# Gate maxima through ScalarE's DMA queue, zero products between the first fold products, and a new instruction order

## The chip, the cores and the metric

The kernel runs on one core of a Trainium2 chip. TensorE (PE) multiplies matrices; VectorE (DVE), ScalarE (ACT) and GpSimd (POOL) do the elementwise work; SyncE (SP) issues nearly all DMA transfers. Each engine works through its own list of instructions in order, and waits where an operand is not ready. The metric is the device time of one execution in microseconds, as a median of several runs.

## The reference, cut to what matters

Three stages follow each other: a gated recurrence over 768 steps for 4 batches of 8 heads, a first feed-forward block, and a second one.

```python
for t in range(S):                       # S = 768, per batch and head, D = 40
    m_new = max(f[t] + m, i[t])          # the running gate maximum
    C = exp(f[t]+m-m_new) * C + exp(i[t]-m_new) * outer(v[t], k[t])
    n = exp(f[t]+m-m_new) * n + exp(i[t]-m_new) * k[t]
    m = m_new
    y[t] = sigmoid(o[t]) * (C @ q[t]) / max(abs(n @ q[t]), 1)
x = y.reshape(3072, 320)
h = ((x @ w1) * (x @ w2)) @ w3           # d_ff = 1024
x = h @ w_out
h = max(x @ v1, x @ v2, x @ v3)          # d_ff = 768
out = h @ v_out
```

The first block multiplies by w3 and then by w_out. Nothing stands between the two, so the kernel computes `w3 @ w_out` once, and uses the product.

## The kernel before, in words

**The recurrence** is cut into chunks of 87 steps, nine per batch (36 in all). A *visit* (`visit`, L817) computes on PE the scores of one chunk (s, L839) and, from the state, the output of the chunk before it (o, L848). VectorE multiplies the scores by a table of decays (`pk`, L873), and the next visit reads the result. The decays of the first nine chunks (`decay`, L744) are made on PE (L757, L758) from the tables `hl` and `one`, and ScalarE takes their exponential (`dd`, L761).

**The gates** come first (L533 to L652). The gate inputs `gi` are loaded, VectorE scans them (L574, L585), joins the chunks (L607, L612) and leaves the maxima in `gft`. These stand with the heads on the partitions, and `hl` wants the chunks there. So they are written to DRAM in three stores (L619) and read back in one load (L650). ScalarE rounds the loaded piece into `hl` (L651) and VectorE adds the remainder (L652). Both DMAs are on SP's queue.

**The fold** (`fold`, L1227) computes `w3 @ w_out` in eight parts of eight products of 320 columns (L1236). The weights arrive as 64-bit floats in *granules* (`granule`, L1154): a DMA, a scaling of the upper word on ScalarE (Prelu, L1172), a shift of the lower word on VectorE (L1181) or on ScalarE (L1178), and a merge on VectorE (L1189). `w_out` has five granules (`wof`, all parts need them), each part has two of w3, and the first of the first part comes in two halves. The landing buffers are four called `sx` and three called `stg`, and the merged halves of w3 go to five buffers `w_0` to `w_4`.

**The rest of PE's work** (L970 to L1102) is the two blocks, in seven blocks of tokens. It starts when the first five chunks are through.

**At the very start** PE multiplies zeros by zeros (`warm`, L508: sixteen, then six more before the first fold product), so that PE is busy while the weights travel.

**What sets the order:** the program is written as a list of operations with their dependencies. A planner (`Plan.run`, L254) plays it with a cost for each operation. Among the operations that are ready on an engine it takes the one with the lowest number in the table `PRIO`, and where an operation may run on either of two engines, the table `PICK` says on which. `WARM` is the time up to which the planner counts PE as slow. What comes out is a fixed list of instructions for each engine.

Of the kernel before, what the change touches and what calls it, by code (L numbers as in the profile page):

```python
# [65 lines left out]
    "11100111101000000100000110110011111101101111000111010011000110011110110011001110001111001011111110110000110010"  # L66
    "00001011101000111101100110011001101110001010010110011101001010110010111001101100101001110001001000001011111011"
    "10100110000001001110000011011110000100011011010111000100110110100000010000000000100100101000010100111101100110"
    "01000100010000101100001100010011010100110011110001011100000110011001110010111000000"
)  # L70
PRIO = (
# [95 lines left out]
)  # L167
WARM = 11500
USTEPS = (
    (0, 1, 3, 5, 8, 11, 14, 18, 22, 26), (0, 2, 4, 6, 8, 11, 14, 17, 20, 23, 26), (0, 2, 4, 6, 8, 9, 11, 12, 14, 15)  # L170
)
# [192 lines left out]
def mlstm_moe_kernel(  # L364
# [133 lines left out]
    def T(*key):  # L498
        v = made[key]
        return v() if callable(v) else v  # L500
# [966 lines left out]
```

## Time and profile before

| | |
|---|---|
| Time before, median of 3 runs | 662.33 us (662.04 to 665.41) |
| The profiled execution | 666.85 us, of which the span is 665.1 us |
| PE busy | 650.4 us, 98% of the span |
| DVE, ACT, POOL busy | 345.7, 296.4, 215.1 us |
| DMA, mean over the span | 114 GB/s |

The span runs from the first instruction to the last. A busy PE can still be slow: the profile also gives the clock that PE was granted. The time between the profiled execution and the median (4.5 us) is no part of any stage, so differences are worked out in the profile and carried over to the median.

### The profile page before, as it was taken

The page shows a single profiled execution, that of the slowest core. Times are in us where ns is not written, and L with a number is a line of the kernel's source. Part 1 is how long each engine was busy: PE and PEld are TensorE (multiplying, and loading weights), DVE is VectorE, ACT ScalarE, POOL GpSimd, SP SyncE. Part 2 cuts the span into 40 slices and gives each one's busy share as a digit, 9 for nine tenths or more (in the row PEclk, how much of TensorE's full clock was granted, in tenths as well). Part 3 has the DMA queues.
Part 4 walks back from the last instruction along what each step waited for, and adds up shares of the span by engine and source line. Part 5 has one row for each costly group of instructions (what it writes and reads, how often), then busy time and mean ns, then how long its engine had stood idle before and what let it go on. Part 6 is the DMA issues. An engine that isn't in the chain of part 4 may idle for free.

```text
span 665.1 us, 14153 instructions
## 1 busy us (share of the span) xinstructions
PE 650.4 (98%) x5903; PEld 575.0 (86%) x5903; DVE 345.7 (52%) x623; ACT 296.4 (45%) x578; POOL 215.1 (32%) x235
## 2 busy tenths in 40 slices
PE   7799999999999999999999999999999999999997
PEld 5477799999999999999999987788788888888896
DVE  5579899877853673554553354464632311332222
ACT  7756986686723353453432343553331122322031
POOL 4053454665512324343244433463300013010030
PEclk9999999999999999999999999999999999999999
DMA  8989964645411444433123244342000010000011
GB/s 277 341 307 369 332 209 150 214 136 186 141 59 62 135 152 147 116 96 90 50 72 104 91 152 127 108 149 65 1 1 1 0 40 1 0 1 0 1 40 39
DMA packets 25457, 75.92 MB, mean 114 GB/s; under 512 B 3145, under 2 KB 6217, under 8 KB 25394
## 3 DMA queue, kind: packets, MB, share of 16 engines
q1 hardware_dynamic: 25394, 75.02, 34.3%
q8 instruction: 46, 0.75, 0.5%
q14 instruction: 17, 0.14, 0.1%
HBM read 70.98 MB, written 4.03 MB: 113 GB/s over the span
## 4 chain that ended last, share of the span: by engine, by line
PE 83%; DVE 5%; DMA 5%; ACT 2%; issue 2%; POOL 1%; SPq 0%; POOLq 0%; ACTq 0%; DVEq 0%
PE wk L970 13%; PE wk L971 13%; PE wk L972 13%; PE wk L973 6%; PE acs L1102 6%; PE wk L975 5%; PE acs L1082 3%; PE acs L1084 3%; PE acs L1086 3%; PE wk L1236 3%; PE aq L848 3%; PE ac L1102 3%; PE aq L839 2%; DMA sx<-in_w3t 2%; PE wk L985 2%
## 5 line engine op out<-in xcount | busy, mean ns | idle before, releaser
L1049 DVE TENSOR_TENSOR misc<-misc,wk 128x384 f32<-128x384 f32 (+2 forms) x87 | 51.3, 594 | 130.5 <-PE wk L975 96.7
L997 ACT CAST hp<-misc 128x384 fp32r<-128x384 f32 (+2 forms) x101 | 55.0, 547 | 141.5 <-DVE misc L1049 53.1
L1001 POOL TENSOR_TENSOR hp<-misc,hp 128x384 fp32r<-128x384 f32 (+1 forms) x40 | 45.6, 1140 | 119.2 <-ACT hp L997 109.3
L970 PE MATMUL wk<-xx,wch 128*128 128x384 f32 (+1 forms) x216 | 77.3, 358 | 0.3 <-DVE misc L1049 0.3
L971 PE MATMUL wk<-xx,wcl 128*128 128x384 f32 (+1 forms) x216 | 76.6, 355 | 0.0
L972 PE MATMUL wk<-xx,wch 128*128 128x384 f32 (+1 forms) x216 | 76.5, 354 | 0.0
L1019 DVE TENSOR_TENSOR misc<-misc,wk 128x384 f32<-128x384 f32 (+1 forms) x56 | 33.8, 607 | 76.8 <-ACT misc L1017 52.2
L970 PE MATMUL wk<-xx,wah 128*128 128x384 f32 (+1 forms) x192 | 69.8, 364 | 0.9 <-DVE misc L1019 0.7
L971 PE MATMUL wk<-xx,wal 128*128 128x384 f32 (+1 forms) x192 | 68.1, 354 | 0.0
L972 PE MATMUL wk<-xx,wah 128*128 128x384 f32 (+1 forms) x192 | 68.0, 354 | 0.0
L1017 ACT COPY misc<-wk 128x384 f32<-128x384 f32 (+1 forms) x56 | 29.2, 522 | 54.7 <-PE wk L975 27.6
L1102 PE MATMUL acs<-wd,hp 128*128 128x320 f32 x234 | 52.7, 310 | 0.1
L1001 POOL TENSOR_TENSOR xx<-misc,hp 128x512 fp32r<-128x512 f32 (+1 forms) x15 | 18.2, 1218 | 95.5 <-ACT hp L997 91.3
L1046 ACT COPY misc<-wk 128x384 f32<-128x384 f32 (+1 forms) x42 | 22.1, 526 | 60.5 <-PE wk L975 45.9
L970 PEld LDWEIGHTS wk<-xx,wch 128*128 128x128 f32 x216 | 40.6, 188 | 3.7 <-DVE misc L1049 0.7
L972 PEld LDWEIGHTS wk<-xx,wch 128*128 128x128 f32 x216 | 40.6, 188 | 3.0
L971 PEld LDWEIGHTS wk<-xx,wcl 128*128 128x128 f32 x216 | 40.6, 188 | 2.9
L1236 PE MATMUL wk<-wof,w 128*128 128x320 f32 x128 | 40.0, 463 | 3.0 <-DVE wof L1189 1.8
L1102 PEld LDWEIGHTS acs<-wd,hp 128*128 128x128 f32 x234 | 39.9, 188 | 1.4 <-ACT misc L1145 0.3
L970 PEld LDWEIGHTS wk<-xx,wah 128*128 128x128 f32 x192 | 36.1, 188 | 4.7 <-DVE misc L1019 1.3
L972 PEld LDWEIGHTS wk<-xx,wah 128*128 128x128 f32 x192 | 36.1, 188 | 2.7
L973 PE MATMUL wk<-xx,wcr 128*128 128x384 f32 (+1 forms) x108 | 38.2, 354 | 0.0
(206 smaller groups left out, 1527.0 us busy)
## 6 DMA issues: line engine op xcount, KB each, us to landing
kv<-in_kv SPq DMA_DIRECT2D x32, 672.0 KB, 4.1
raw<-in_qk SPq DMA_DIRECT2D x36, 348.0 KB, 4.2
dd<-d_na SPq DMA_DIRECT2D x24, 348.0 KB, 3.8
sx<-in_w3t SPq DMA_DIRECT2D x9, 512.0 KB, 7.5
stg<-in_wc SPq DMA_DIRECT2D x9, 512.0 KB, 4.6
out<-misc SPq DMA_DIRECT2D x24, 160.0 KB, 1.9
stg<-in_w3t SPq DMA_DIRECT2D x6, 512.0 KB, 10.5
sx<-in_wa SPq DMA_DIRECT2D x6, 512.0 KB, 8.4
```

What stands on the lines that cost most here:

```text
L970: PE.matmul(p, lhsT=h_[:, kt], rhs=xh[:, kt], start=kt == 0, stop=False)
L971: PE.matmul(p, lhsT=l_[:, kt], rhs=xh[:, kt], start=False, stop=False)
L972: PE.matmul(p, lhsT=h_[:, kt], rhs=xl[:, kt], start=False, stop=False)
L973: PE.matmul(p, lhsT=r_, rhs=xh[:, 2], start=False, stop=False)
L975: PE.matmul(p, lhsT=r_, rhs=xl[:, 2], start=False, stop=True)
L997: P.op("A", act(n), lambda sl=sl: A.copy(out=T("ph", key)[:, sl], in_=T(*src)[:, sl]), r=[src + part], w=[("ph", key) + part])
L1001: e.tensor_tensor(out=T("pl", key)[:, sl], in0=T(*src)[:, sl], in1=T("ph", key)[:, sl].bitcast(F32), op=ALU.subtract)
L1017: P.op("A", act(n, True), lambda: A.copy(out=T(*sa), in_=T(*ps[0])), r=[ps[0]], w=[sa])
L1019: P.op("V", dve(n), lambda: V.tensor_tensor(out=T(*sa), in0=T(*sa), in1=T(*ps[1]), op=ALU.mult), r=[ps[1]], w=[sa])
L1049: P.op("V", dve(sl.stop - sl.start), lambda sl=sl: V.tensor_tensor(out=T(*sc)[:, sl], in0=T(*sc)[:, sl], in1=T(*ps)[:, sl], op=ALU.max), r ...
L1102: PE.matmul(T(f"ac{m}", (k, 1)), lhsT=src[:, m * 128:m * 128 + 128], rhs=w[:, o:o + DM], start=first_, stop=last_,)
L1236: PE.matmul(T(*ps), lhsT=T(*w3)[:, i * 128:i * 128 + 128], rhs=wof[:, gt * 320:gt * 320 + 320], start=gt == 0, stop=gt == 7,)
```

## The change

Four edits. The stores and the load of the gate maxima are issued from ScalarE, all three stores in one operation and the load in another. Of the zero products, sixteen remain at the start and four before the first fold product, and one follows each of the first five fold products. `PRIO` and `PICK` are new tables, and `WARM` is 8000 instead of 11500. The w_out granules and the first w3 granules have another order by these tables, and so has everything behind them.

```diff
@@
-    "11100111101000000100000110110011111101101111000111010011000110011110110011001110001111001011111110110000110010"
...
+    "10100000010010001010110001100011010000111100011101011100110100101001010111001110011001100101100111100001001100"
...
-WARM = 11500
+WARM = 8000
@@
+    def zeros(n):
+        for i in range(n):
+            PE.matmul(T("so", -1)[:, i % 2 * 512:i % 2 * 512 + 512], lhsT=wb[:, NA - 1, 512:640],
+                      rhs=wb[:, NA - 1, 0:512], start=True, stop=True)
@@
-    for n, dep in ((16, ()), (6, (("wo", 0, 0),))):
...
+    for n, dep in ((16, ()), (4, (("wo", 0, 0),))):
+
+        fill.append((mm(512) * n, lambda n=n: zeros(n), 512 * n, dep))
@@
-    for i in range(3):
-        dma(100, lambda i=i: SP.dma_start(
-            out=d_na[0, 3 * i:3 * i + 3].rearrange("c h t -> h c t"), in_=c3(T("g", "gft"))[32 * i:32 * i + 8]
-        ), r=[("g", "gft")], w=[("dna", 0, i)])
+    def f():
+        for i in range(3):
+            A.dma_start(out=d_na[0, 3 * i:3 * i + 3].rearrange("c h t -> h c t"), in_=c3(T("g", "gft"))[32 * i:32 * i + 8])
+
+    P.op("A", 1050, f, r=[("g", "gft")], w=[("dna", 0)], early={(("dna", 0), None): -2200})
+    P.op("A", 350, lambda: A.dma_start(out=raw_v, in_=d_na[0, :, :, 0:L]), r=[("dna", 0)], w=[("rv", 0)],
+         early={(("rv", 0), None): -2200})
@@
-    dma(150, lambda: SP.dma_start(out=raw_v, in_=d_na[0, :, :, 0:L]), r=[("dna", 0)], w=[("rv", 0)])
@@
+                if (ft, gt) < (0, 5):
+                    zeros(1)
@@
-                P.op("P", 537.5 * m, lambda w3=w3, q=q, gts=gts: products(w3, q, gts), cols=1280 * m,
-                     r=[*(("wo", 0, i) for i in wos), w3 + ((g0 // 2,) if n < 512 else ())], w=[ps])
+                z = (ft, g0) < (0, 5)
+                P.op("P", 537.5 * m + mm(512) * z, lambda w3=w3, q=q, gts=gts: products(w3, q, gts),
+                     cols=1280 * m + 512 * z, w=[ps] + [("so", -1)] * z,
+                     r=[*(("wo", 0, i) for i in wos), w3 + ((g0 // 2,) if n < 512 else ()), *[("wb", NA - 1)] * z])
```

The order of instructions, at the three places that the prediction speaks of. On SP, the first transfers of the kernel before (`in_wo` is w_out, `in_gi` the gates, `in_og` a table for the first outputs; the number of a buffer follows its name):

```order
L1167 DMA sx_0_97<-in_wo 128x1024
L1167 DMA stg<-in_w3t 128x512
L533 DMA misc<-in_gi 96x522
L1167 DMA sx_1_98<-in_wo 128x1024
L1167 DMA sx_2_99<-in_wo 128x1024
L1167 DMA stg<-in_w3t 128x512
L1167 DMA sx_0_100<-in_wo 128x1024
L1167 DMA sx_0_97<-in_w3t 128x1024
L1167 DMA stg<-in_wo 128x1024
L1167 DMA sx_1_98<-in_w3t 128x1024
L619 DMA d_na<-misc 8x3x87 x3
L1167 DMA sx_2_99<-in_w3t 128x1024
```

And of the changed kernel:

```order
L1170 DMA stg<-in_w3t 128x512
L537 DMA misc<-in_gi 96x522
L1170 DMA sx_0_97<-in_wo 128x1024
L1170 DMA stg<-in_w3t 128x512
L1170 DMA sx_1_98<-in_wo 128x1024
L1170 DMA sx_0_100<-in_wo 128x1024
L1170 DMA sx_2_99<-in_wo 128x1024
L1170 DMA stg<-in_wo 128x1024
L1170 DMA sx_0_97<-in_w3t 128x1024
L667 DMA sg_86<-in_og 96x1600
L1170 DMA sx_1_98<-in_w3t 128x1024
L792 DMA raw_1_107<-in_qk 128x696
```

The gates are second instead of third, all five w_out granules stand before the third granule of w3, `in_og` stands before the next w3 granule, and the stores are gone. On ACT, from the gates to the first merge, of the kernel before:

```order
L604 COPY misc<-misc 32x3x87 x3
L1172 ACTIVATE sx_1_98<-sx_1_98 128x512
L1178 ACTIVATE sx_2_99<-sx_2_99 128x512
L1172 ACTIVATE sx_2_99<-sx_2_99 128x512
L1172 ACTIVATE stg<-stg 128x256
L1178 ACTIVATE stg<-stg 128x256
L640 CAST hl_83<-misc 32x1152
L1172 ACTIVATE sx_0_100<-sx_0_100 128x512
L1178 ACTIVATE sx_0_97<-sx_0_97 128x512
L1172 ACTIVATE sx_0_97<-sx_0_97 128x512
L1178 ACTIVATE sx_0_100<-sx_0_100 128x512
L1172 ACTIVATE stg<-stg 128x512
```

And of the changed kernel (L621 are the stores, L624 the load, L654 the rounding into `hl`):

```order
L603 COPY misc<-misc 32x3x87 x3
L1175 ACTIVATE sx_0_97<-sx_0_97 128x512
L1175 ACTIVATE stg<-stg 128x256
L644 CAST hl_83<-misc 32x1152
L621 DMA d_na<-misc 8x3x87 x3
L1175 ACTIVATE sx_1_98<-sx_1_98 128x512
L1175 ACTIVATE sx_0_100<-sx_0_100 128x512
L1175 ACTIVATE sx_2_99<-sx_2_99 128x512
L624 DMA misc<-d_na 9x696
L1175 ACTIVATE stg<-stg 128x512
L1175 ACTIVATE sx_0_97<-sx_0_97 128x512
L654 CAST hl_84<-misc 9x8x87
```

The shifts (L1178) have gone from this stretch to VectorE, and the stores, the load and the rounding now stand between the scalings of the granules. On PE, from the zeros to the first decay, of the kernel before:

```order
L541 MATMUL aq_0_112<-wb 128x512 x22
L659 MATMUL ac_114<-cs,misc 127x32 x9
L1236 MATMUL wk_0_109<-wof,w_0_101 128x320 x4
L1236 MATMUL wk_0_109<-wof,w_1_102 128x320 x4
L1236 MATMUL wk_1_110<-wof,w_2_103 128x320 x4
L1236 MATMUL wk_1_110<-wof,w_3_104 128x320 x4
L839 MATMUL aq_0_112<-raw_0_106 87x87 x8
L757 MATMUL wk_0_109<-hl_84,hl_83 128x352
```

And of the changed kernel, from its last zeros in a row to the first score (the products of the first part's first half, with a zero product behind each, stand just before):

```order
L509 MATMUL aq_0_112<-wb 128x512
L1239 MATMUL wk_0_109<-wof,w_1_102 128x320 x3
L760 MATMUL wk_2_111<-hl_84,hl_83 128x352
L761 MATMUL wk_2_111<-one 128x352
L1239 MATMUL wk_1_110<-wof,w_2_103 128x320 x4
L760 MATMUL wk_0_109<-hl_84,hl_83 128x352
L761 MATMUL wk_0_109<-one 128x352
L1239 MATMUL wk_1_110<-wof,w_3_104 128x320 x4
L760 MATMUL wk_2_111<-hl_84,hl_83 128x352
L761 MATMUL wk_2_111<-one 128x352
L842 MATMUL aq_0_112<-raw_0_106 87x87 x8
```

The decays now stand between the halves of the second part and ahead of the first score, where they stood behind both.

## Rows read from the trace of the kernel before

**Rows 1.** The page: busy time of each engine, share of the span, instructions.

```profile
PE 650.4 (98%) x5903; PEld 575.0 (86%) x5903; DVE 345.7 (52%) x623; ACT 296.4 (45%) x578; POOL 215.1 (32%) x235
```

**Rows 2.** Who waited for whom, PE: total us, times, longest us.

```profile
PE wk L1236 <- DVE wof L1189: 1.8, 2, 1.6
PE wk L757 <- DVE hl L652: 1.6, 1, 1.6
```

**Rows 3.** Stretches: length, busy PE, PEld, DVE, ACT, POOL, granted clock, DMA share, GB/s.

```profile
6.00:8.00 2.00, 2.00 (x9) 1.58 (x8) 1.79 (x5) 1.02 (x3) 0.37 (x2) 1.00 1.00 388
...
14.00:16.00 2.00, 2.00 (x5) 0.83 (x3) 0.33 (x1) 0.83 (x2) 0.60 (x1) 0.50 0.98 293
...
31.00:32.00 1.00, 1.00 (x3) 0.67 (x2) 0.99 (x2) 1.00 (x3) 0.00 (x0) 0.50 1.05 415
...
14.00:45.00 31.00, 26.50 (x236) 17.99 (x238) 17.99 (x33) 21.19 (x41) 5.96 (x6) 0.90 0.92 317
45.00:89.00 44.00, 42.70 (x604) 34.66 (x592) 40.17 (x81) 35.05 (x74) 17.98 (x17) 1.00 0.92 333
```

**Rows 4.** Timeline of PE: start, length, instruction, count, idle before and releaser.

```profile
12.49 3.67 PE L1236 MATMUL wk<-wof,w 128*128 128x320 f32 x8 [0.30 <-DVE w L1189]
17.76 1.34 PE L1236 MATMUL wk<-wof,w 128*128 128x320 f32 x4 [1.60 <-DVE wof L1189]
19.31 5.65 PE L1236 MATMUL wk<-wof,w 128*128 128x320 f32 x20 [0.21 <-DVE wof L1189]
...
27.34 0.43 PE L757 MATMUL wk<-hl,hl 128*128 128x352 f32 x1 [1.60 <-DVE hl L652]
...
29.92 6.26 PE L1236 MATMUL wk<-wof,w 128*128 128x320 f32 x16 [0.73 <-ACT dd L761]
...
38.91 0.85 PE L839 MATMUL acs<-raw 40*87 40x87 f32 x16
...
45.55 4.54 PE L1236 MATMUL wk<-wof,w 128*128 128x320 f32 x16 [0.20 <-ACT stg L1172]
```

**Rows 5.** Timeline of SP's queue, DMA issues.

```profile
10.65 0.33 SPq L1167 DMA_DIRECT2D sx<-in_w3t  x1
11.52 1.10 SPq L619 DMA_DIRECT2D d_na<-misc  x3
...
18.06 0.29 SPq L650 DMA_DIRECT2D misc<-d_na  x1
```

**Rows 6.** Timeline of ACT.

```profile
15.17 0.67 ACT L1178 ACTIVATE sx<-sx 128x512 int32<-128x512 uint16 x1 [1.90 <-DMA sx<-in_w3t]
...
16.28 0.65 ACT L1178 ACTIVATE sx<-sx 128x512 int32<-128x512 uint16 x1
...
24.88 0.77 ACT L651 CAST hl<-misc 9x696 fp32r<-9x696 f32 x1
```

**Rows 7.** Timeline of DVE.

```profile
6.76 0.69 DVE L574 TENSOR_TENSOR_SCAN misc<-misc 96x261 f32<-96x261 f32 x1
...
12.83 1.50 DVE L646 TENSOR_TENSOR hl<-misc,hl 32x1152 fp32r<-32x1152 f32 x1
...
21.71 0.69 DVE L1189 SCALAR_TENSOR_TENSOR w<-sx 128x512 int32<-128x512 int32 x1 [0.36 <-ACT sx L1172]
```

**Rows 8.** DMA issues: queue, count, KB each, us from issue to landing.

```profile
sx<-in_w3t SPq DMA_DIRECT2D x1, 512.0 KB, 6.6
sx<-in_w3t SPq DMA_DIRECT2D x1, 512.0 KB, 7.5
sg<-in_og SPq DMA_DIRECT2D x1, 600.0 KB, 10.9
...
out<-misc SPq DMA_DIRECT2D x24, 160.0 KB, 1.9
```

**Rows 9.** One tile's instructions (`sx`, first 60 us): count, shortest, median, longest ns.

```profile
L1178 ACT ACTIVATE sx<-sx x9: 654/667/675, 9.8 to 59.6; 128x512 int32<-128x512 uint16 x9
...
L1181 DVE TENSOR_SCALAR sx<-sx x6: 399/428/433, 4.7 to 56.3; 128x512 int32<-128x512 int32 x6
```

More of the change, by code (lines that the diff above doesn't have):

```diff
@@ L65 @@
 PICK = (
-    "11100111101000000100000110110011111101101111000111010011000110011110110011001110001111001011111110110000110010"
-    "00001011101000111101100110011001101110001010010110011101001010110010111001101100101001110001001000001011111011"
-    "10100110000001001110000011011110000100011011010111000100110110100000010000000000100100101000010100111101100110"
-    "01000100010000101100001100010011010100110011110001011100000110011001110010111000000"
+    "10100000010010001010110001100011010000111100011101011100110100101001010111001110011001100101100111100001001100"
+    "01011101010001111011111110010001110110110111111111001111111111000001010100000100111001011010110010101011000101"
+    "11100010111111100000000011101011010010100000011100100010110010100100010001010011000110000111000110101011001111"
+    "11110100001110001010000001100000000011010100000010010000101100111011001011001000000"
 )
 PRIO = (
[95 rows of a table removed]
[94 rows of a table added]
 )
-WARM = 11500
+WARM = 8000
 USTEPS = (
@@ L536, in mlstm_moe_kernel @@
     new(("so", -1), [128, 1024], F32, "aq")
-    for n, dep in ((16, ()), (6, (("wo", 0, 0),))):
-        def f(n=n):
-            for i in range(n):
-                PE.matmul(T("so", -1)[:, i % 2 * 512:i % 2 * 512 + 512], lhsT=wb[:, NA - 1, 512:640],
-                          rhs=wb[:, NA - 1, 0:512], start=True, stop=True)
-        fill.append((mm(512) * n, f, 512 * n, dep))
+    for n, dep in ((16, ()), (4, (("wo", 0, 0),))):
+        fill.append((mm(512) * n, lambda n=n: zeros(n), 512 * n, dep))
     warm(0)
@@ L617, in mlstm_moe_kernel @@
     ), r=[("mp", 0, 0), ("mp", 0, 1)], w=[("g", "aug", 0)])
-    for i in range(3):
-        dma(100, lambda i=i: SP.dma_start(
-            out=d_na[0, 3 * i:3 * i + 3].rearrange("c h t -> h c t"), in_=c3(T("g", "gft"))[32 * i:32 * i + 8]
-        ), r=[("g", "gft")], w=[("dna", 0, i)])
+    raw_v = T("rv", 0)[64:64 + NCH].rearrange("p (a b) -> p a b", b=L)
+    def f():
[4 more added lines that the diff above has]
+         early={(("rv", 0), None): -2200})
     P.op("G", 400, lambda: G.memset(T("hl", 1)[64:128].bitcast(F32), 0.0), w=[("hl", 1, 2), ("hl", 1, 3)])
@@ L648, in mlstm_moe_kernel @@
     P.op("V", dve(NCH * 128), f, r=[("g", "aug"), ("hl", 0, 0)], w=[("hl", 0, 1)])
-    hi, raw_v = T("hl", 1)[64:64 + NCH, :, 0:L], T("rv", 0)[64:64 + NCH].rearrange("p (a b) -> p a b", b=L)
-    dma(150, lambda: SP.dma_start(out=raw_v, in_=d_na[0, :, :, 0:L]), r=[("dna", 0)], w=[("rv", 0)])
+    hi = T("hl", 1)[64:64 + NCH, :, 0:L]
     P.op("A", act(8 * L), lambda: A.copy(out=hi, in_=raw_v), r=[("rv", 0)], w=[("hl", 1, 2)])
```

189 rows, old and new, of the table PRIO are left out of this document.

## The prediction

> **What bounds the kernel now.** I read the page's busy times first, then who PE waited for, then the stretches, and last the timelines of the first 45 us. PE is busy for 98% of the span [rows 1], so only three things can make the kernel shorter: less work on PE, fewer waits of PE, or a faster clock while it works. The change takes no product of the computation away. The two longest waits of useful work are for a w_out granule (1.8 us in two waits) and for the table `hl` (1.6 us) [rows 2]. The stretches say where to look. From 14 to 45 us PE is busy for 26.50 of 31.00 us at a mean clock of 0.90; from 45 to 89 us for 42.70 of 44.00 us at full clock [rows 3]. What can be won lies ahead of 45 us.
>
> There I add up what PE lost against the rate of a later stretch, where 16 fold instructions (8 products) take 4.54 us, or some 0.55 us a product [rows 4]:
> - From 12.49 to 17.76 us it did 4 products, worth 2.2 us, in 5.3 us: 3.1 us lost, half of it to waiting (1.60) and half to a granted clock of 0.50, the 1.2 GHz level [rows 3, 4].
> - From 17.76 to 19.31 us it did 2 products, worth 1.1: 0.45 us lost [rows 4].
> - The waits of 1.60 us at 27.34 and of 0.73 us at 29.92: 2.3 us [rows 4].
> - The 16 instructions from 29.92 took 6.26 instead of 4.54 us, again at a clock of 0.50: 1.7 us [rows 3, 4].
>
> Together 7.6 us. More than that cannot be won here.
>
> Why did these waits come? ACT takes its list in order. The fourth w_out granule's shift (16.28) stood behind the shift of a w3 granule that landed only at 15.17 [rows 6]. And the gate maxima made a long trip: stored from 11.52, load issued at 18.06, rounded at 24.88 [rows 5, 6]: 13.4 us.
>
> **The change part by part.** Times for the changed kernel are estimates from these rows.
>
> *Gates.* They are issued second instead of third on SP, behind 256 KB instead of 768 KB, and VectorE's scan (at 6.76 [rows 7]) has no granule ahead of it. I put the scan at 4.8 us and, with the rest of the chain as long as now, the stores at 9.4 instead of 11.52. On its own this gives PE nothing; it starts the trip.
>
> *The trip on ACT's queue.* Each DMA costs ACT issue time. SP needs 1.10 us for the three stores and 0.29 for the load [rows 5], so ACT loses 1.4 us that SP gains. No row shows a DMA on another queue than SP's. The bounds are two landings at the shortest landing that the page has, 1.9 us [rows 8], plus the issues, so 5.2 us, and the 13.4 us of now. I take 6.5, near the low end, because what stretches the trip now is what stands ahead on SP: its w3 granules took 6.6 and 7.5 us to land [rows 8]. Then `hl` is rounded at about 16 us and complete at 18 us on VectorE instead of 27.3. The wait of 1.60 us goes, and decays can fill PE while it waits for granules.
>
> The Trainium skill speaks for this and against it in one page. "DMA: Bandwidth & Descriptors", section "Queues, rings and completion order", says that each DMA engine takes turns between the queues that have work; then a short transfer on ACT's empty queue need not wait for SP's backlog, and the sum is the one below. Its section "Issuing engines are not separate DMA queues" says that DMAs from several engines run on the same 16 DMA engines and interleave, and that only issue time is saved; by that the trip stays at 13.4 us, which is the second rival below. No run here shows which one holds.
>
> *w_out ahead of w3.* The five w_out granules are merged at some 9, 13, 14, 15 and 15.8 us, each held by VectorE's own list: the 1.50 us of the `hl` subtraction [rows 7] stands ahead of the second. The waits for `wof` go, and what is late next is the third w3 piece, which stays at about 17 us: its buffer is freed by the first merge, which comes at about the same time as now. So the first part is done at 19.4 instead of 20.4 us (19.31 and two products): a gain of 1.0.
>
> The second part gets later. Its w3 granule is issued when the buffer of the second w_out granule is free, at 13.0 instead of 10.65 us [rows 5]; with 6.6 us to land [rows 8] it is merged at 20.6. The next one waits on SP for a lane and for a buffer until 15.3, lands after 8 us and is merged at 25.0, against 22.4 now (21.71 and 0.69 [rows 7]). That puts the fold back by 2.6 us. Two pairs of decays lie in that gap, and they had to be done anyway. Bounds for that landing from the rows: 6.6 and 10.9 us [rows 8], so the merge at 23.6 to 27.9.
>
> *From there to the second visit.* In the trace the second visit's scores start at 38.91 [rows 4]. In the new order 32 fold products instead of 28 and one pair of decays more come ahead of it, 2.5 us of work that is then done. I count for the changed kernel: first product at 10.6; 32 products 17.2 us, one visit 0.8, six pairs of decays 2.3, zeros 1.1; waits of 1.8 (second w_out granule), 1.6 (third w3 piece), 0.7, 1.5 (the two w3 granules) and 0.5 (the first visit's input): 38.5 us. So 0.4 us earlier with 2.5 us more done: **2.9 us won**. With the bounds of the landing it is 0 to 4.3.
>
> *Zero products.* The nine that are left near the fold cost 0.22 us each (nine in 2.00 us [rows 3]), where six stood before. The first four of the single ones stand ahead of a wait for a granule, which hides them; the fifth is on the path. At half the clock it is 0.4. I take 0.2, which is in the 1.1 above. Do they hold the clock? It fell after stretches with idle PE, and the pieces are too short to fill the waits of 1.6 and 1.8 us; I count nothing for it. A fall between 20 and 30 us would cost at most the 1.7 us that it costs now, a clock that stays up gains nothing beyond the sum.
>
> *Tables.* By the new `PICK` VectorE does seven more shifts ahead of the eighth visit's `pk` (20 instead of 13), at 0.43 us [rows 9] 3.0 us; its other lines there add and drop a few, which I put at +1: 4.0 us more. ACT does nine shifts fewer by then, at 0.67 us [rows 9], 6.0 us less. VectorE's cover is its idle time: 13.0 us from 14 to 45 us (31.00 less 17.99), but only 3.8 from 45 to 89 (44.00 less 40.17) [rows 3]. To carry the 2.9 us on, 6.9 of the 13.0 must be used up. My count of its waits up to the second visit leaves about 6 us, so it just holds. Behind 89 us I take no difference.
>
> **The sum:** 666.85 (profiled execution: 665.10 span and 1.75 around it) less 2.9 is 663.95. The median of the runs stands 4.5 us below the profiled execution; with the same difference, 662.33 less 2.9 is **659.4 us**.
>
> **Rivals.**
> 1. *The next waits don't come.* If the granules land as fast as the fastest did, the fold is never late and the 7.6 us go except for the zeros (1.1): 6.5 won, 655.8 us. For it: 317 GB/s from 14 to 45 us against 388 at 6 to 8 [rows 3], so the transfers have room. Against it: two buffers are freed later than now.
> 2. *The trip is as slow on ACT's queue.* Then `hl` is rounded at 22.8 us, and ACT, in order, holds the scalings of both w3 granules of the second part behind it: they are merged at 27 and 29 instead of 20.6 and 25.0. That is 4.0 us on the path, 1.1 more than was won: 663.4 us.
> 3. *VectorE becomes the bound* (the other side). If its waits ahead of 45 us are set by landings and stay as long as they are, its 4.0 us more have no cover, the `pk` that each visit waits for comes 4.0 us later, and PE waits as long: 666.3 us. It decides from the point where VectorE's idle time from 14 to 45 us stays above 9.0 us (13.0 less 4.0). For it: 91% busy from 45 to 89 us, with no room to catch up. Against it: the 13.0 us of idle time, and the 6.0 us that ACT gets rid of.
> 4. *The zeros don't do what they are there for* and the clock falls in a stretch that is on the path: 1.7 us less won, 661.1.
>
> **How the numbers follow.** My forecast 0.48 (its own range 657.5 to 661.5), rival 1 0.21, rival 2 0.11, rival 3 0.17, rival 4 0.03. Within 0.5% (3.3 us, about what a measurement of this kernel can tell from no change) lies 659.0 to 665.6. Of the forecast's 0.48 I put 0.20 below 659.0; with rival 1 that is 0.41 for faster. Rival 3 gives 0.13 above 665.6 and 0.04 below, rival 2 0.02 above: 0.15 for slower. The rest, 0.44, is the same. The range that leaves out 2 in 10 goes from 655.3, just under rival 1, to 665.6, under the end of rival 3.
>
> **What would show it.** Right: the load's rounding on ACT at about 16 us, `hl` off the list of PE's waits, the first fold part done by 19.5, the second visit's scores at 38 to 39 us behind 32 fold products, VectorE's idle time from 14 to 45 us near 6. Wrong: the rounding after 20 us (rival 2); PE waiting on VectorE's `pk` or `misc` between 45 and 120 us (rival 3); PE's waits for w3 merges ahead of 30 us under 2 us in all (rival 1); a clock of 0.50 in a stretch behind 20 us (rival 4). The whole is wrong if the difference comes from behind 140 us, where I expect none.

## The result: slower by 0.75%, and the profile after

The changed kernel takes 668.3 us, median of 6 runs (667.59 to 670.50), against 664.1 us of the kernel before in the same series (6 runs): a ratio of 1.0075, 95% interval 1.005 to 1.010. Later series put the kernel before at 664.0 to 664.9 us. Forecast were 659.4 us, with 15% for slower.

The page's busy times and the stretches of the changed kernel, beside [rows 1, 3] (stretch columns as there):

```profile
PE 651.0 (98%) x5906; PEld 576.6 (87%) x5906; DVE 349.7 (53%) x639; ACT 294.9 (44%) x575; POOL 200.1 (30%) x222
```
```profile
14.00:45.00 31.00, 28.55 (x185) 20.20 (x186) 20.94 (x40) 19.06 (x37) 2.56 (x2) 0.89 0.91 309
45.00:89.00 44.00, 40.21 (x629) 32.38 (x628) 41.18 (x80) 31.99 (x66) 14.57 (x18) 1.00 0.85 314
```

PE looks busier from 14 to 45 us than before, but part of that are the new zero products. From 45 to 89 us it stands still for 3.8 us (44.00 less 40.21), where it was 1.3.

The trip of the gate maxima on ACT's queue (ACTq are its DMA issues), and what stands behind it in ACT's list, beside [rows 6]:

```profile
10.49 1.20 ACTq L621 DMA_DIRECT2D d_na<-misc  x3
11.74 1.80 ACT L1175 ACTIVATE sx<-sx 128x512 f32<-128x512 f32 x3 [1.36 <-DVE w L1192]
17.76 0.28 ACTq L624 DMA_DIRECT2D misc<-d_na  x1
18.09 0.66 ACT L1175 ACTIVATE stg<-stg 128x512 f32<-128x512 f32 x1 [4.55 <-DMA d_na<-misc]
18.65 0.68 ACT L1175 ACTIVATE sx<-sx 128x512 f32<-128x512 f32 x1
20.72 0.77 ACT L654 CAST hl<-misc 9x696 fp32r<-9x696 f32 x1 [1.39 <-DMA misc<-d_na]
```

Stores at 10.49, load at 17.76, rounding at 20.72: 10.2 us. ACT issues the load itself, so it stands for 4.55 us until the stores have landed. Behind it are the scalings of the last w_out granule (18.09) and of the third piece of w3 (18.65).

VectorE's merges, SP's issues and PE over the same time:

```profile
13.57 0.69 DVE L1192 SCALAR_TENSOR_TENSOR wof<-sx 128x512 int32<-128x512 int32 x1
...
18.78 0.69 DVE L1192 SCALAR_TENSOR_TENSOR wof<-stg 128x512 int32<-128x512 int32 x1 [2.64 <-ACT stg L1175]
...
19.91 0.69 DVE L1192 SCALAR_TENSOR_TENSOR w<-sx 128x512 int32<-128x512 int32 x1
...
23.87 0.69 DVE L1192 SCALAR_TENSOR_TENSOR w<-sx 128x512 int32<-128x512 int32 x1 [0.52 <-ACT sx L1175]
```
```profile
9.76 0.33 SPq L1170 DMA_DIRECT2D sx<-in_w3t  x1
10.13 0.43 SPq L667 DMA_DIRECT2D sg<-in_og  x1
14.29 0.33 SPq L1170 DMA_DIRECT2D sx<-in_w3t  x1
```
```profile
14.32 0.81 PE L1239 MATMUL wk<-wof,w 128*128 128x320 f32 x2 [1.99 <-DVE wof L1192]
...
20.66 0.81 PE L1239 MATMUL wk<-wof,w 128*128 128x320 f32 x2 [2.13 <-DVE w L1192]
...
30.17 0.85 PE L842 MATMUL aq<-raw 40*87 40x87 f32 x16
...
40.79 0.85 PE L842 MATMUL acs<-raw 40*87 40x87 f32 x16
```

I count the pieces of w3 as merged: two halves, then whole granules (the third is `w_1`). The third is merged at 20.6 us (19.91 + 0.69), the fourth, whose transfer went out at 14.29, at 24.6. PE's two waits end with the second w_out merge (13.57 + 0.69) and with the third piece's; behind 20.66 it doesn't stand again before 45 us, though it ran at half its clock from 22 to 24 us. The second visit's scores start at 40.79, not at the 38.91 of [rows 4].

The profiled execution of before was a poor base. A second trace of the kernel before (664.29 us, near its median) has the same order and an earlier second visit. Its granted clock from 30 to 34 us, its fourth merge and its second visit:

```profile
30.00:34.00 4.00, 4.00 (x17) 2.96 (x16) 3.73 (x7) 3.96 (x9) 0.92 (x1) 1.00 1.03 410
```
```profile
18.68 0.69 DVE L1189 SCALAR_TENSOR_TENSOR w<-sx 128x512 int32<-128x512 int32 x1
```
```profile
36.10 0.85 PE L839 MATMUL acs<-raw 40*87 40x87 f32 x16
```

The clock there is 1.00, where the profiled execution shows 0.57:

```profile
30.00:34.00 4.00, 4.00 (x9) 2.64 (x10) 2.86 (x5) 4.00 (x9) 0.00 (x0) 0.57 1.04 416
```

So the same program reaches its second visit at 36.1 or at 38.9 us. The changed kernel, at 40.79, is 4.7 us behind this run and not 1.9; 2.5 us of that is useful work which it has already done (32 fold products and six pairs of decays ahead of these scores, where before it was 28 and five).

**One row per kernel.** All kernels of this study, each from its one trace. Merges are ends on VectorE; "rest" is the span less the start of the second visit's scores; the last column is the time in which PE stood from 45 to 89 us.

| kernel | ratio, 95% interval | 4th, 5th piece merged | second visit | span | rest | PE idle 45 to 89 |
|---|---|---|---|---|---|---|
| before, second trace | 1 | 19.4, 21.8 | 36.10 | 662.6 | 626.5 | 1.5 |
| before, profiled execution | | 19.9, 22.4 | 38.91 | 665.1 | 626.2 | 1.3 |
| before_act | 1.0015 (0.9995 to 1.0036) | 20.5, 23.1 | 40.69 | 666.4 | 625.7 | 0.7 |
| before_copies | 1.0053 (1.0032 to 1.0073) | 18.9, 25.0 | 39.23 | 664.8 | 625.6 | 1.6 |
| before_w4late | 1.0107 (1.0083 to 1.0132) | 25.6, 26.7 | 43.16 | 669.0 | 625.8 | 1.2 |
| after (the change) | 1.0075 (1.005 to 1.010) | 24.6, 27.1 | 40.79 | 665.8 | 625.0 | 3.8 |
| after_nozero | 1.0076 (1.0052 to 1.010) | 24.4, 27.0 | 40.36 | 665.2 | 624.8 | 3.8 |
| after_sp | 1.0044 (1.0027 to 1.0061) | 23.0, 25.5 | 38.82 | 664.7 | 625.9 | 3.4 |
| after_hl84 | 1.0047 (1.0031 to 1.0063) | 21.3, 23.8 | 39.26 | 665.1 | 625.8 | 3.5 |
| after_sp84 | 1.0032 (1.0018 to 1.0046) | 22.4, 25.1 | 40.11 | 665.0 | 624.9 | 3.8 |
| after_spall | 1.0034 (1.0017 to 1.0051) | 21.3, 24.1 | 39.10 | 664.0 | 624.9 | 3.7 |
| after_both | 1.0058 (1.0038 to 1.0078) | 23.7, 26.2 | 42.68 | 667.4 | 624.7 | 2.8 |
| after_hl83 | 1.0078 (1.0056 to 1.010) | 25.6, 29.1 | 42.56 | 667.1 | 624.5 | 2.8 |
| after_copies | 1.0067 (1.0041 to 1.0093) | 24.0, 27.1 | 41.44 | 666.5 | 625.1 | 3.4 |
| after_cast | 1.009 (1.0066 to 1.0115) | 20.6, 26.4 | 42.99 | 668.7 | 625.7 | 2.7 |
| after_late | 1.0137 (1.0114 to 1.0159) | 26.3, 28.8 | 44.16 | 670.0 | 625.8 | 2.7 |
| after_pool | 1.0161 (1.0141 to 1.0182) | 29.2, 31.7 | 46.66 | 672.5 | 625.8 | 2.7 |

The column "rest" is the first finding: over 17 traces the second visit starts between 36.1 and 46.7 us, and what follows takes 624.5 to 626.5 us. Within a set of lists, nothing lost ahead of that point is given back behind it. The second visit follows the merge of the fifth piece by 13 to 18 us; that is no rule, as the kernel before alone shows 14.3 and 16.5.

The last column is the second finding. All 12 kernels with the new lists come to the second visit with the same 2.5 us more useful work done, and yet their rest is only 0.7 us shorter in the mean (625.3 against 626.0). From 45 to 89 us PE stands for 2.7 to 3.8 us in each of the 12, and for 0.7 to 1.6 in each of the five with the old ones, whatever was done to the trip. So part of the loss lies behind the second visit. The second trace of the kernel before, then `after_spall` (below), in which most of the early loss is undone:

```profile
45.00:89.00 44.00, 42.52 (x643) 34.80 (x642) 39.26 (x77) 34.94 (x74) 18.16 (x16) 1.00 0.88 316
```
```profile
45.00:89.00 44.00, 40.26 (x637) 32.78 (x638) 41.16 (x79) 33.20 (x69) 14.50 (x19) 1.00 0.83 308
```

The clock alone doesn't explain the loss: `after_spall` has 1.00 from 10 us to its second visit and is slower than the second trace of before, with 0.93 in the mean.

### The profile page after: what moved, and what is told of

The parts are those of the page before. It is cut to its first block, busy times and chain, and to the rows that moved or that the text cites. A ratio compares the mean times of both kernels' runs of the same rounds, so it can differ in the third digit from the quotient of the medians.

```text
span 665.8 us, 14151 instructions
## 1 busy us (share of the span) xinstructions
PE 651.0 (98%) x5906; PEld 576.6 (87%) x5906; DVE 349.7 (53%) x639; ACT 294.9 (44%) x575; POOL 200.1 (30%) x222
## 4 chain that ended last, share of the span: by engine, by line
PE 88%; DVE 5%; DMA 3%; ACT 2%; issue 1%; POOL 0%; SPq 0%; ACTq 0%; DVEq 0%
PE wk L973 14%; PE wk L974 14%; PE wk L975 14%; PE wk L976 7%; PE acs L1105 6%; PE wk L978 5%; PE acs L1085 3%; PE aq L851 3%; PE acs L1089 3%; PE acs L1087 3%; PE ac L1105 3%; PE aq L842 3%; PE wk L1239 3%; DMA sx<-in_w3t 2%; PE wk L988 2%; PE ac L1085 2%
## 5 line engine op out<-in xcount | busy, mean ns | idle before, releaser
L1004 POOL TENSOR_TENSOR hp<-misc,hp 128x384 fp32r<-128x384 f32 (+1 forms) x43 | 49.2, 1146 | 122.3 <-ACT hp L1000 96.8
L1004 POOL TENSOR_TENSOR xx<-misc,hp 128x512 fp32r<-128x512 f32 (+1 forms) x17 | 19.7, 1164 | 99.4 <-ACT hp L1000 79.3
L973 PEld LDWEIGHTS wk<-xx,wah 128*128 128x128 f32 x192 | 36.1, 188 | 4.5 <-ACT dd L764 1.1
L809 POOL TENSOR_TENSOR pk<-kv,dd 63x696 f32<-63x696 f32 (+1 forms) x15 | 25.7, 1712 | 45.2 <-PE aq L851 26.7
L975 PEld LDWEIGHTS wk<-xx,wah 128*128 128x128 f32 x192 | 36.1, 188 | 2.7
```

The lines of the kernel that those rows point to most:

```text
L973: PE.matmul(p, lhsT=h_[:, kt], rhs=xh[:, kt], start=kt == 0, stop=False)
L975: PE.matmul(p, lhsT=h_[:, kt], rhs=xl[:, kt], start=False, stop=False)
L1004: e.tensor_tensor(out=T("pl", key)[:, sl], in0=T(*src)[:, sl], in1=T("ph", key)[:, sl].bitcast(F32), op=ALU.subtract)
```

## The experiments

**The first question: who stands for the trip?** Theory 1 was that ACT's own wait costs the time; theory 2 blames the new lists. In `after_pool` stores and load are issued by GpSimd, all else as changed:

```diff
-            A.dma_start(out=d_na[0, 3 * i:3 * i + 3]...
+            G.dma_start(out=d_na[0, 3 * i:3 * i + 3]...
-    P.op("A", 350, lambda: A.dma_start(out=raw_v, ...
+    P.op("A", 350, lambda: G.dma_start(out=raw_v, ...
```

> The changed kernel with the three stores and the load issued from GpSimd, which has nothing to do there; every other engine's list is the same word for word. Theory 1 (ScalarE, in order, waits 4.6 us for its own stores and 1.4 us for its load, and holds up the merges of w_out and w3, by them SP's next loads, by them the fold): those waits go, the second half of the first fold part starts near 17 us instead of 20.7, and the time falls by 3 to 4 us against the changed kernel, to 664 to 665 us. Theory 2 (the new tables cost the time: VectorE has more to do ahead of the eighth visit, and PE waits for it between 45 and 89 us): the early gain is given back there, less than 1 us is won, 667 to 668.

In `after_late` the load stays on ACT, two instructions later:

```diff
         for t, j, fn in order:
+            if j == self.late:      # the load
+                held = [fn, 2]
+                continue
             fn()
+            if held and pick[j][0] == "A":
+                held[1] -= 1
+                if held[1] == 0:
+                    held[0]()
```

> The changed kernel with the load two instructions later on ScalarE, behind the scalings of the fifth w_out granule and of the third w3 piece; nothing else moves. The round trip stays as long. Theory 1: the two merges come at 15 to 16.5 us instead of 19.5 to 20.6, the fold's first part ends near 19.5, SP's next load is issued 3 us earlier; 1.5 to 2.5 us less than the changed kernel, 665.5 to 666.5. Theory 2: no more than 0.5 us.

The forecasts of both theories fell: 674.7 and 674.0 us, slower than the change by 4 to 6 us (ratios 1.0161 and 1.0137 against 1.0075). ACT's wait at the load was gone and came back longer, at the rounding. Neither run takes away the waits behind 45 us that theory 2 names. `after_pool`, SP's issues, then ACT, then VectorE:

```profile
17.29 0.43 SPq L792 DMA_DIRECT2D raw<-in_qk  x1
29.21 0.33 SPq L1170 DMA_DIRECT2D sx<-in_w3t  x1
```
```profile
25.36 0.77 ACT L654 CAST hl<-misc 9x696 fp32r<-9x696 f32 x1 [8.17 <-DMA misc<-d_na]
```
```profile
26.16 0.88 DVE L655 TENSOR_TENSOR hl<-misc,hl 9x696 fp32r<-9x696 f32 x1 [8.24 <-ACT hl L654]
```

ACT and VectorE stand for 8.2 us before the two rows that make `hl`. Behind these are the w3 pieces whose merges would free buffers, so SP hands out nothing from 17.7 to 29.2 us, and the DMA engines run dry (share 0.10, 38 GB/s):

```profile
24.00:30.00 6.00, 1.71 (x4) 1.07 (x5) 2.58 (x5) 4.62 (x9) 0.00 (x0) 0.66 0.10 38
```

The load itself took longer, too: issued at 19.39, its data there at 25.36. Freed of its wait, ACT had released buffers, and SP had put four large transfers (15.83 to 16.81 and 17.29) ahead of the load. In `after_late` it took from 18.06 to 22.46, with two w3 granules more ahead of it than in the changed kernel (17.76 to 20.72).

**The zeros** (`after_nozero`): no single zero products between the fold products.

```diff
-        (the five single zero products between the first fold products)
```

> The changed kernel without the five single zero products between the first fold products; the lists are else the same. Theory 3 (the zeros cost or save something by themselves): if they hold the clock, the time rises by 1 us or more; if they only stand in the way, it falls by 0.3 to 1. Theories 1 and 2: within 0.3 us of the changed kernel, because each of the first four stands ahead of a wait for a granule.

669.8 us, ratio 1.0076: as the change. Costs or savings under some 1.7 us (0.25%, half of either interval) can't be told here, and none above that shows.

**A second look at the kernel before** (`before_again`), one run with a profile: 664.29 us; its rows stand above.

> The kernel before, unchanged, for a second trace of it, since its first profiled execution (666.85 us) was slower than each of its six timed ones. If the executions differ by falls of TensorE's clock, this one has a stretch at 0.50 more or less than the first, and its span follows: about 662 to 665 us. Every theory expects the waits of 45 to 89 us as in the first.

**Lists by queue.** `before_act` sends the old lists' stores and load from ACT's queue, `after_sp` the new lists' from SP's:

```diff
-        dma(100, lambda i=i: SP.dma_start(out=d_na[0, ...    (before)
+        dma(100, lambda i=i: A.dma_start(out=d_na[0, ...
```
```diff
-            A.dma_start(out=d_na[0, ...                      (changed kernel)
+            SP.dma_start(out=d_na[0, ...
```

> The kernel before, all lists as they were, but its three stores and its load go from ACT's queue instead of SP's. Theory 3: ACT stands for the stores' landing at the load (some 3 us), behind it pieces of w3 that free buffers; SP no longer stands itself; 663 to 667 us. Theory 4: no change or a little faster (no new lists): 662 to 664 us.

> The changed lists with stores and load on SP's queue, as the kernel before has them; with before, before_act and after it makes a table of lists by queue. SP stands at the load for the stores' landing (from 11 to 15 us or later) ahead of the fourth w3 granule's transfer. Theory 5: 668 to 672 us, since that granule comes later still. Theory 6: less is in flight ahead of stores and load, hl lands some 2 us sooner than in the changed kernel: 666 to 667 us. If the queue were the cause, this kernel would be at 664 to 665 us.

| median, us | SP's queue | ACT's queue |
|---|---|---|
| old lists | 664.0 to 664.9 | 665.7 |
| new lists | 667.5 | 668.3 |

The queue is worth about 1 us (0.15%, interval touching 0, on the old lists; 0.3% by the ratios on the new ones, intervals overlapping); the lists are worth about 3. `before_act` lies in theory 3's 663 to 667. `after_sp` missed theory 5's 668 to 672 by half a microsecond, theory 6's 666 to 667 as well, and the queue as the cause (664 to 665) by more. SP hardly stood: its stores went out ahead of the next w3 granule and had landed when it came to the load, 1.5 us after the last of them (10.89 + 1.03 to 13.37).

```profile
10.89 1.03 SPq L621 DMA_DIRECT2D d_na<-misc  x3
12.01 0.36 SPq L1170 DMA_DIRECT2D sx<-in_w3t  x1
12.42 0.43 SPq L667 DMA_DIRECT2D sg<-in_og  x1
13.37 0.29 SPq L624 DMA_DIRECT2D misc<-d_na  x1
```

**A trip without DRAM.** `after_copies` and `before_copies` replace it by nine copies from tile to tile, one landing instead of two:

```diff
+            for c in range(3):
+                SP.dma_start(out=raw_v[3 * i + c:3 * i + c + 1], in_=c3(T("g", "gft"))[32 * i:32 * i + 8, c:c + 1])
```

> The changed kernel, but the trip through DRAM is replaced by nine copies (one row of 8 x 87 each) from the gates' tile straight to the row layout, issued by SP behind in_og, so that one landing stands where stores and load had two, and ACT neither issues nor waits for them. Theory 3 (what costs is that ACT and VectorE stand before the two parts of hl while the trip lands, so that the weights' buffers aren't freed and the weights' transfers stop): hl some 3 us earlier, ACT's waits of 4.55 and 1.39 us gone, SP not held 20.4 to 24.6; 660 to 663 us. Theory 4 (the new lists load VectorE more between 45 and 89 us, and the trip is a side matter): 666 to 668 us.

> The kernel before with the same nine copies on SP in place of its three stores and its load. Theory 3: SP isn't held from 15.5 to 18.6 us and TensorE's wait of 1.0 to 1.6 us for hl goes; 661 to 663 us. Theory 4: about 663 us, too. The two copies kernels together tell what the new lists are worth without the trip: by theory 3 they lie within 1 us or the changed lists are faster, by theory 4 the changed lists are 3 to 5 us slower.

Both missed (669.9 and 667.9 us). In the changed lists `hl` was rounded at 19.24, 1.5 us sooner, but the nine issues kept SP for 7.15 us in both kernels, and in that time no weights were handed out:

```profile
10.77 7.15 SPq L631 DMA_DIRECT2D misc<-misc  x9
18.02 0.38 SPq L1180 DMA_DIRECT2D sx<-in_w3t  x1
```

The two kernels lie 2.0 us apart, between theory 3 (within 1) and theory 4 (3 to 5). An experiment that exchanges one hold for another tells little about the lists; nor does it show what a sooner `hl` is worth by itself.

**Rows put elsewhere in the changed lists.** These kernels emit each engine's list as planned, with single operations moved by so many places (`rows`: the list of each engine; the dependencies are kept):

```diff
+        for j, k in self.move:
+            r = rows[pick[j][0]]
+            at = [o for o, _ in r].index(j)
+            r.insert(at + k, r.pop(at))
```

`after_cast` has the load two places later and the rows for `hl` later on ACT (8) and VectorE (3), but not on PE. Theory 3 (the stopped transfers of the weights cost the time) against theory 4 (VectorE's load behind 45 us):

> As after_late (the load on ACT's queue two instructions later), and besides the two parts of hl stand later: ACT's behind eight more of its instructions (output gates, the wb of the first pair, three prelus or conversions of w3 pieces), VectorE's behind three more, so that neither engine stands before them while the load lands. Theory 3: SP's hold, 18.5 to 26.3 us in after_late, shortens by 3 us or more and so does the time: 668 to 671 us. Theory 4: 673 to 675 us, as after_late, since TensorE has its hl no sooner.

671.1 us: at the upper end of theory 3's range, 3 us better than `after_late`; theory 4's 673 to 675 fell. PE then stood for 3.87 us at its first product with `hl`. In `after_hl84` that product goes behind the fourth and fifth piece as well, as the old lists have it; `after_hl83` moves the rows of the gates' other tile behind the w_out pieces, and by that one w_out scaling goes ahead of ACT's stores; `after_both` does both:

```diff
+    P.move = [(20, 2), (26, 8), (27, 5), (92, -1), (97, -2)]    # after_hl84
+    P.move = [(24, 4), (50, -1), (25, 8), (59, 2)]              # after_hl83
```

> The changed kernel with the load two instructions later on ACT (as in after_late), and all that needs what the trip brings put where the kernel before has it, behind the fourth and fifth w3 granule: ACT's conversion of hl, VectorE's subtraction, and TensorE's first products with hl. Nothing stands and waits for the trip ahead of w3 work. Theory 5: the 3.9 us that TensorE waited for hl in after_cast are filled with two groups of the fold; 666 to 668 us. Theory 6: hl lands at 22 to 24 us as in after_cast, so 670 to 672 us.

> The changed kernel with the two parts of the other gates' tile (hl_83: ACT's conversion, VectorE's subtraction, 1.15 and 1.44 us) put behind the w_out pieces that they stood ahead of, so that a w_out buffer is merged and given to the fourth w3 granule sooner. Theory 5 (what decides is how many w3 granules are decoded by 24 us; the changed lists have two fewer there, since the gates' rows stand ahead of the pieces that free the buffers): that granule's transfer goes out at 11.6 to 12.5 us instead of 14.3, but ACT still stands at its load to 18 us: 667 to 668 us. Theory 6 (what decides is when hl lands, whatever the weights do): no change, 668 to 669 us.

> Both sets of moves of after_hl83 and after_hl84. Theory 5: w3 granules four and five are merged 2 us or more sooner than in after_hl84, and most of what the change lost is back: 664 to 666 us. Theory 6: 670 to 672 us.

667.3, 669.0 and 668.3 us. The first agrees with theory 5 (667.3 in 666 to 668) and not with theory 6. PE has its fold pieces at once:

```profile
21.36 4.94 PE L1249 MATMUL wk<-wof,w 128*128 128x320 f32 x16 [0.37 <-DVE w L1202]
```

Of the other two, `after_hl83` shows no change, as theory 6 said (668 to 669) and theory 5 did not; `after_both` missed both. SP handed out the fourth piece at 12.42 (`after_hl83`) and 12.68 (`after_both`) instead of 14.29, as meant. But in `after_hl83` ACT stood for its load as before (4.11 us), and the subtraction that I had moved now ran between the last w_out merge and the third piece's, just where PE waited. VectorE, then PE:

```profile
18.68 0.69 DVE L1202 SCALAR_TENSOR_TENSOR wof<-stg 128x512 int32<-128x512 int32 x1 [4.08 <-ACT stg L1185]
19.40 1.35 DVE L660 TENSOR_TENSOR hl<-misc,hl 32x1152 fp32r<-32x1152 f32 x1
20.78 0.43 DVE L1194 TENSOR_SCALAR sx<-sx 128x512 int32<-128x512 int32 x1
21.32 0.69 DVE L1202 SCALAR_TENSOR_TENSOR w<-sx 128x512 int32<-128x512 int32 x1
```
```profile
22.06 1.44 PE L1249 MATMUL wk<-wof,w 128*128 128x320 f32 x2 [6.38 <-DVE w L1202]
```

In `after_both` the stores had landed only at 20.34, 8.5 us after the last of them (10.60 + 1.19): the granule that went out sooner travelled beside them. ACT stood at the load with the fourth piece's scaling behind it.

**One transfer moved, from the side of the kernel before** (`before_w4late`): old lists, SP's queue; the fourth piece's transfer alone goes six places back in SP's list.

```diff
+    P.move = [(90, 6)]
```

> The kernel before, its lists on TensorE, VectorE, ACT and GpSimd unchanged; on SP one transfer alone is moved: that of the fourth w3 granule (sx_1_98, handed out at 10.8 us) goes behind the stores, the next w3 granule, in_og and in_qk, so at about 15 us, which is where the changed lists hand it out (14.3). Theory 5 (the time at which this granule is merged sets the second visit's scores, and these set the end): merged at 22 to 24 us instead of 19.4, the second visit's scores 2 to 3 us later, 666 to 667.5 us, though the stores then land sooner. Rival theory 7 (what the changed lists lose comes from the gates' rows put ahead on ACT and VectorE and from the work moved onto VectorE after 45 us, not from this transfer): 664 to 665 us, no change.

672.2 us, ratio 1.0107. Theory 7's forecast of no change is out, and theory 5's size was too small. The other half of theory 7, that work moved onto VectorE costs time behind 45 us, isn't tested by this run: it has the old lists there. The transfer went out at 14.92 instead of 10.80, and the engines take their lists in order. VectorE, ahead of the last w_out merge, stands for the piece, and SP cannot go on (8.46 us for two issues). SP, VectorE and PE:

```profile
14.92 0.35 SPq L1177 DMA_DIRECT2D sx<-in_w3t  x1
16.99 0.30 SPq L660 DMA_DIRECT2D misc<-d_na  x1
17.50 8.46 SPq L1177 DMA_DIRECT2D sx<-in_w3t  x2
```
```profile
23.98 0.43 DVE L1191 TENSOR_SCALAR sx<-sx 128x512 int32<-128x512 int32 x1 [6.51 <-DMA sx<-in_w3t]
```
```profile
25.06 7.79 PE L1246 MATMUL wk<-wof,w 128*128 128x320 f32 x20 [6.19 <-DVE wof L1199]
```

4.1 us on one transfer became 6.2 us on the fourth merge and, with a clock at half for longer than in the second trace of before (0.80 against 0.93 in the mean from 10 to 36 us), 7.1 us on the second visit.

**All of it undone in the changed lists.** `after_sp84` is `after_sp` with the moves of `after_hl84` but for the load's; `after_spall` adds those of `after_hl83` and lets the load stand behind the fourth piece's transfer.

> The changed lists with stores and load on SP's queue (as after_sp) and what needs the trip behind the fourth and fifth w3 granule (as after_hl84). Theory 5: the fourth granule merges by 21 us and TensorE doesn't wait, the second visit's scores at 37 to 38.5 us; 664 to 666 us, about as the kernel before or a little faster, since the changed lists leave about 1 us less to do from there. Theory 7: no better than after_sp and after_hl84 by themselves, 667 to 668 us.

> The changed lists with all of it undone that theory 5 names: stores and load on SP's queue (the load behind the fourth w3 granule's transfer), the rows of hl_83 behind the w_out pieces, all that needs the trip behind the fifth w3 granule. Theory 5: the fourth granule's transfer at 12.5 to 13.5 us instead of 14.5 in after_sp84, its merge by 21 us, the second visit's scores at 38 to 39 us, 664 to 666 us: what the change lost is back, and nothing is won. Rival theory 8 (the fold is bound by the DMA engines, whatever the order): the scores at 40 us as in after_sp84, 666.5 to 668 us.

666.8 and 666.7 us, each 0.7 to 0.8 us above theory 5's range: a little over half of the loss is back (1.0032 and 1.0034 against 1.0075 for the change), where all of it was expected. Theory 7's 667 to 668 for `after_sp84` was missed by 0.2. Theory 8's range held the time of `after_spall`, though its scores came at 39.10 instead of 40, nearer to theory 5. Its fourth and fifth pieces are still merged at 21.3 and 24.1, 1.9 and 2.3 us behind the second trace of before, and the second visit is 3.0 us behind. But 2.5 us of useful work and three zero products more stand ahead of that visit, so little or nothing is lost there any more; its rest is 1.6 us shorter (624.9 against 626.5) instead of 2.5. None of the kernels beats the kernel before.

## Why the prediction was wrong, point by point

**Two steps failed, and the base was off.** Against the profiled execution of before, the second visit was to come at 38.5 us and came at 40.79: 2.3 us too late. The rest was to be 2.5 us shorter and was 1.2 shorter (625.0 against 626.2): 1.3 us more. Together the span is 0.7 us longer instead of 2.9 shorter. The median is 4.2 us longer; the other 3.4 are the executions that were profiled, 2.7 us above its median for the kernel before (666.85 against 664.1) and 0.7 below it for the changed one.

**The first step that failed is the trip on ACT's queue.** It was put at 6.5 us and took 10.2 (10.49 to 20.72), from 5.2 to 13.4 allowed. Two things were missing in it.
- *A new queue was taken to be free of what stands ahead on SP's.* It wasn't. The three stores, 24 KB in all, were issued by 11.69 and had landed only at 17.76, six microseconds later, on a queue with nothing else in it. SP had just handed out 1.1 MB (9.76 and 10.13). In `after_sp` they landed within 1.5 us with nothing handed out since the last w_out granule at 4.52. On SP's queue behind a granule handed out at 10.65 they took 5.4 us in the kernel before (12.62 to the load at 18.06 [rows 5]). So in these runs the landing goes with the bulk in flight around it and not with the queue. "DMA: Bandwidth & Descriptors" of the Trainium skill, section "Issuing engines are not separate DMA queues", says that only issue time is saved; by that rule the queue changes little, and the table of lists by queue agrees. The rule on turns between queues (the Trainium skill, the same page, section "Queues, rings and completion order"), on which I had leaned, would have let the stores through; the 6 us speak against using it so here.
- *The load's own wait was priced as issue time alone.* I charged ACT 1.4 us for issuing and named nothing that stood behind the load. Behind it stood the last w_out scaling and the third piece's: "the third w3 piece, which stays at about 17 us" was merged at 20.6.

**Gates second.** Stores at 9.4 were forecast, 10.49 measured: VectorE's scan came at 5.51 instead of 4.8, and two granules' merges and GpSimd's strips lie between it and the end. This put the trip back by 1.1 us.

**w_out ahead of w3.** The first part was to be done at 19.4 and ended near 24 us. The next two merges, forecast at 20.6 and 25.0, came at 24.6 and 27.1, though PE, at half its clock from 22 to 24 us, reached the fourth piece only at 25.01 and did not stand for either; the forecast issue at 13.0 was at 14.29, since the second w_out merge came at 13.57. Ahead of that merge stood ACT's stores (11.74 is the scaling's start) and VectorE's subtraction for the other gates' tile. With stores and subtraction behind that piece (`after_hl83`) the transfer goes out at 12.42.

**The second visit.** Forecast 38.5 us with 2.5 us more done, measured 40.79. The terms of that sum, as listed, add up to 38.1; with 0.55 us a product the 32 products are 17.6 and not 17.2, which gives the 38.5, and with 4.54 for eight they are 18.2. The work was done: 32 fold products and the decays stand ahead of it. But the rest is only 1.2 to 1.5 us shorter (625.0 against 626.2 and 626.5), because PE waits 2.3 to 2.5 us more from 45 to 89 us; 0.9 to 1.1 less behind that gives part of it back. The waits there, PE's in us, times, longest:

```profile
PE wk L760 <- DVE wb L1266: 1.3, 2, 1.1
PE wk L973 <- ACT dd L764: 1.0, 1, 1.0
PE wk L1239 <- DVE wb L1266: 0.8, 1, 0.8
PE wk L927 <- ACT dd L764: 0.6, 1, 0.6
```

**The tables are the second step that failed.** That VectorE's idle time would cover its additional work was needed to carry the 2.9 us on. I needed this idle time from 14 to 45 us down to 6; it was 10.1 (31.00 less 20.94), above the 9.0 from which rival 3 was to decide. That rival forecast the right difference (4.0 us), in part by luck: PE's waits on VectorE did come, but for `wb` above, 2.1 us, and not for the `pk` of each visit; 1.6 us more are ACT's `dd`, and the other part of the loss lies ahead of the second visit. Of the 12 traces with the new lists, 11 show 2.1 to 2.2 us for `wb` from 45 to 89 us and `after_sp` 1.3; the five with the old lists show none.

**Rival 2**, the slow trip, had the mechanism: rounding at 22.8 (20.72), merges at 27 and 29 (24.6 and 27.1), and priced it at a loss of 1.1 against the kernel before, so 663.4. It stopped short of the third piece, which was held as well, and its base was too low.

**The base.** The sum was made against an execution that reached its second visit 2.8 us later than the second trace of the same kernel, for the most part, as I read the two traces, by the clock at 0.50 ([rows 3], 31 to 32 us; 1.7 us in my own sum) and longer waits for `wof` and `hl`. So the 4.5 us between that execution and the median, which I took for no part of any stage, lie for a good part ahead of the second visit, and less than the 7.6 us that I added up could be won in a typical run. The median to which I carried the sum (662.33, of 3 runs) was low, too, by about 2 us.

**Right was** that nothing is to be counted on the zeros for the clock: it fell to 0.50 in the changed kernel as well, from 22 to 24 us among others. Without the single ones the time is the same within what can be told, so the 0.2 us that I gave them is neither shown nor refuted.

```profile
22.00:24.00 2.00, 2.00 (x6) 1.20 (x5) 1.41 (x4) 1.99 (x4) 0.00 (x0) 0.50 0.98 379
```

Right, too, that `hl` leaves PE's waits, and nearly that nothing behind 140 us matters (0.4 us less idle PE from 140 to 600 us).

**What is open:** the last 2 us of `after_spall`. By its trace they lie behind the second visit: PE waits 2.3 us more from 45 to 89 us than in the second trace of before (42.52 less 40.26), for the same `wb` and `dd` as the changed kernel. That the work which `PICK` gave to VectorE makes these late is argued: no run gave it back. So a little over half of the loss is shown by runs to come from the trip and the order around it; the other half is located, and its cause stays open.

## What to carry to other kernels

Before a DMA is moved to a computing engine's queue, list what stands behind its wait on that engine, and which buffers that work frees; the wait costs what those buffers feed. In these runs short stores landed within 1.5 us with little in flight and after 5.4 to 8.5 us behind bulk, from SP's queue as from ACT's: try to issue them while little is in flight before another queue. And take a second trace of the kernel before as the base when a few microseconds are at stake, look for one late point behind which all traces take equally long, and count the work done ahead of it, since a list that has done more there owes a shorter rest.

## What I had not expected of the hardware

- The same program, with the same lists, had its clock at 0.57 or 1.00 from 30 to 34 us in two executions, after PE had waited for 2.7 us (1.60 and 0.73 [rows 4], and 0.36 at 28.62) or 2.1 us (0.97, 0.37 and 0.72 in the second trace).
- Nine copies between tiles of 2.8 KB each kept SP for 7.1 us, 0.79 us an issue, in both kernels; three stores took 1.03.
- A clock of 1.00 through the whole of 10 to 46 us (`after_sp84`, `after_spall`) did not make the kernel faster than the one before, whose clock in the second trace was 0.50 from 14 to 16 us.
